# Moving the softmax's exponential, the blocks' transfers and the wo products by a slot in a fused attention and MLP kernel

## The chip, the cores and the metric

The kernel runs on one core of a Trainium2 chip. The metric is the device time of one execution in microseconds, as the median of several runs. Engines are named as in the profile: PE (TensorE matmul), PEld (TensorE weight load), DVE (VectorE), ACT (ScalarE), POOL (GpSimd) and SP (SyncE, which issues most DMAs).

## The reference

The input x has 2048 rows of 576 values, in float32. Two branches read the same normalized rows and are added to x: sliding attention with 32 heads of 18 values, in which each row looks at itself and seven rows before it in steps of two, and an MLP of 4608 hidden values with relu.

```python
xn = layernorm(x)
qkv = (xn @ wqkv).reshape(B, S, 3, 32, 18)              # q, k, v by head
idx = pos[:, None] - arange(8) * 2                      # rows s, s-2, ..., s-14
logits = where(idx >= 0, q . k[idx] * 18 ** -0.5, -1e9)
o = softmax(logits) . v[idx]
return x + o.reshape(B, S, 576) @ wo + maximum(xn @ w1, 0) @ w2
```

## The kernel before

**Tiling and phases.** The rows are dealt out in two phases (even and odd rows, so that the dilated window becomes a plain one). A phase has 8 tiles of 128 rows, and two tiles make a block of 256 rows (`tb`). The 4608 hidden values are 12 chunks (`c`) of three groups of 128 (`f`, C = 3). One slot is one combination (phase, chunk, block, f): 144 slots a phase, 288 in all, `n` in the code. A slot of the steady state has half of the hidden products of two slots (`h_two`: first half at even n, second half at odd n, then ReLU on ScalarE into `hhi` and the remainder on VectorE into `hlo`), and the output products of its own (`o_two`, into four PSUM tiles `po`). At f = 2 VectorE adds the four `po` tiles to x (line 702), and the next slot, with f = 0, uses the same tiles again. Every value is split into a high and a low float32r part, so that weights pass through a staging tile `st`, a ScalarE copy (line 161) and a VectorE subtraction (line 165): a *split*. `run_splits` does the splits that are due and calls `stage_more`, which keeps three more loads under way (`AHEAD`) in five staging buffers.

**Attention.** Heads are taken in four units of 8 heads, 24 slots apart. `qkv_tile` puts the q, k, v products of one tile into one slot, eight slots a unit. After that `attention` fills a queue `bg` of VectorE work: products q*k and their sums, the mask on GpSimd after the last sum, then maximum, subtraction, exponential (ScalarE, in the same function as the subtraction), sum, reciprocal, division, and the products with v and their sums. At the end of each slot `run_bg` takes work from that queue as long as VectorE's planned clock `t["dve"]` isn't past TensorE's planned clock `t["pe"]` by more than `margin(n)`. Both clocks are the kernel's own bookkeeping when it is built; they only set the order of instructions.

**The wo products.** In chunk 10 the attention's output tiles are transposed: `wo_a` transposes 32 by 32 blocks on VectorE and sends them by four DMAs to DRAM (`blocks_out`), `wo_f` reads them back in turned order (tile `xn`), `wo_s` splits them, and `o_two` takes wo's products in the slot with f = 1 of that block. `WO_STEPS` holds the slots for `wo_a`, `wo_f` and `wo_s`.

**The change of phase.** During chunk 11 of the first phase the second phase's first four tiles go the same way (`XT_STEPS`: load, statistics, `norm_turned`, `xt_a`, `xt_f`, `xt_s`); the last four are normalized by `stats` and `norm` and transposed on TensorE (`make_xt`).

**What sets the order.** Each engine runs its instructions in the order of the program. Work is put into a slot's list by `at` (before the slot's output products) or by `late` (after them, before `run_bg`). SP's DMAs stand in one queue in the order of the same calls: an issue that waits for its data or its buffer holds up all that follow. The pools that matter: `ph` and `pm` two PSUM tiles each, `po` four, `st` five, `pr` two, `tr` two, `xn` three.

Of the kernel before, what the change touches and what calls it, by code (L numbers as in the profile page):

```python
# [18 lines left out]
P = 128  # L19
# [7 lines left out]
C = 3  # L27
# [5 lines left out]
WO_CHUNK = 10  # L33

XT_STEPS = (
    (-6, 0, 1, 2, 4, 7),
    (-5, 1, 2, 3, 5, 8),
    (-3, 2, 3, 4, 6, 10),
    (3, 4, 5, 6, 8, 11),
)  # L40
WO_STEPS = ((-5, -4), (-3, -3), (-1, -1))
HEADW = (-9, -8, -7, -6, -5, -4)
FIRST = 4

# [14 lines left out]
def tile_body(ctx: ExitStack, tc: tile.TileContext, x, wqkv, wo, w1, w2, out):  # L59
# [61 lines left out]
    def mm_rows(runs, behind=None):  # L121


        if behind is not None:
            tc.add_manual_dep(nc.tensor.nop().ins, behind.ins.name, SYNC, reason="PSUM banks change rows")
        for pair in zip(*runs, strict=True):
            for z, (o, l, r, start, stop, n) in zip((slice(0, 64), slice(64, P)), pair):
                ins = nc.tensor.matmul(o, l[z], r[z], start=start, stop=stop)  # L128
            t["pe"] += pair[0][5] / 2400.0 + 0.002
        return ins  # L130

    def dve(n):
# [2 lines left out]

    tasks = deque()
    staged = deque()
    AHEAD = 3

    def split_task(step, load, split):  # L140
        tasks.append((step, load, split))

    def stage_more(ahead=AHEAD):
        while tasks and len(staged) < ahead:
            step, load, split = tasks.popleft()
            st = stp.tile([P, 640], F32, name="st")
            load(st)
            staged.append((step, split, st))
# [200 lines left out]
    LOWER, LOWER_MORE = FULL_K + [(4, 4)], FULL_K + [(4, 4), (4, 9)]  # L349
    UPPER, UPPER_MORE = FULL_K + [(4, 4)], FULL_K + [(4, 4), (9, 9)]  # L350

    def blocks_out(td, tr):
        for r in range(4):
            rows = slice(32 * r, 32 * r + 32)
            nc.sync.dma_start(  # L355
                td[:, :, rows].rearrange("g j i -> j g i"),
                tr[rows, :].rearrange("j (g i) -> j g i", i=32),
            )
# [8 lines left out]
    def xt_a(ph, i):  # L367

        xn, tr = XN.pop((ph, i))
        nc.vector.transpose(tr, xn)  # L370
        dve(D)
        TD[ph, i] = turned.tile([D // 32, 32, P], F32, name="words")
        blocks_out(TD[ph, i], tr)

    def xt_f(ph, i):
        tb, h = divmod(i, 2)
        if h == 0:
            XT[ph, tb] = xtp.tile([P, 10, TBN], F32R, name="xT")
        z, td = f32(XT[ph, tb][:, 0:5, h * P : (h + 1) * P]), TD.pop((ph, i))
        nc.sync.dma_start(z[:, 0:KT], td[0 : 4 * KT].rearrange("(k c) j i -> (c j) k i", k=KT))  # L380
        for rows in slice(0, DR), slice(DR, P):
            nc.sync.dma_start(z[rows, KT], td[4 * KT : D // 32].rearrange("c j i -> (c j) i"))
# [21 lines left out]
    def qkv_tile(ph, u, i):  # L404

        if u == 0 and i == 0:
            QO[ph] = qop.tile([P, NI, D], F32, name="qo")
        if i == 0:
            assert len(bg) < 38, len(bg)
            KK[ph, u] = kp.tile([P, W - 1 + NI, UD], F32, name="k")  # L410
            VV[ph, u] = vp.tile([P, W - 1 + NI, UD], F32, name="v")
            nc.gpsimd.memset(KK[ph, u][0:1, 0 : W - 1, :], 0.0)
            nc.gpsimd.memset(VV[ph, u][0:1, 0 : W - 1, :], 0.0)
        k, v, wq = KK[ph, u], VV[ph, u], WQ[ph, u]
        tb, second = i // 2, i % 2 == 1
        xt = XT[ph, tb]

        def run(h, terms):
            return [
                (PQ[h], xt[:, a, h * P : (h + 1) * P], wq[:, b, :], not second and j == 0, second and j == len(terms) - 1, 3 * UD)  # L420
                for j, (a, b) in enumerate(terms)
            ]

        if not second:
            for h in range(2):
                PQ[h] = ps_m.tile([P, 3, UD], F32, name="pm")
            PQ[2] = mm_rows((run(0, LOWER_MORE), run(1, UPPER_MORE)))
            return
        mm_rows((run(1, LOWER), run(0, UPPER)), PQ[2])
        for h in range(2):  # L430
            j, pq = i - 1 + h, PQ.pop(h)
            nc.scalar.activation(k[:, W - 1 + j, :], pq[:, 1, :], AF.Copy)  # L432
            nc.scalar.activation(v[:, W - 1 + j, :], pq[:, 2, :], AF.Copy)
            nc.scalar.activation(QO[ph][:, j, u * UD : (u + 1) * UD], pq[:, 0, :], AF.Copy)
        if i == NI - 1:
            for z in (k, v):
                for a, b in HALO:
                    nc.scalar.dma_start(z[a + 1 : b + 1, 0 : W - 1, :], z[a:b, NI : NI + W - 1, :])
# [8 lines left out]
    def attention(ph, u):  # L447
# [28 lines left out]

        def sm_sub():
            nc.vector.tensor_tensor(lg, lg, spread(m), op=ALU.subtract)
            nc.scalar.activation(lg, lg, AF.Exp, scale=scale)

        def sm_sum():
# [23 lines left out]
        for i in range(0, NI, 2):  # L505
            for f in (qk_mul, qk_sum):
                for j in (i, i + 1):
                    bg.append((big, f, (j,)))
        for f in (sm_max, sm_sub, sm_sum, sm_rcp, sm_div):
            bg.append((n + 130, f, ()))  # L510
        for i in range(0, NI, 2):
            for j in (i, i + 1):
                bg.append((big, av_mul, (j,)))
# [2 lines left out]
                    bg.append((w * UD, av_add, (j, w)))  # L516

    def run_bg(margin):
        while bg and t["dve"] + bg[0][0] / 960.0 <= t["pe"] + margin:
            n, f, a = bg.popleft()  # L520
            f(*a)
            dve(n)


    OT = {}
# [1 line left out]
    def wo_a(ph, i):  # L527


        assert (ph, i) in ready, (ph, i, len(bg))  # L530
        o = QO[ph][:, i, :]
        tr = tmp.tile([P, 640], F32, name="tr", bufs=2)
        nc.vector.transpose(tr[:, 0:D], o)
        nc.vector.transpose(tr[:, D:640], o[:, KT * P : D])
        dve(D)
        dve(DR)
        TD[ph, i] = turned.tile([5 * 4, 32, P], F32, name="turned")
        blocks_out(TD[ph, i], tr)

    def wo_f(ph, i):  # L540
        OT[ph, i] = tmp.tile([P, 5, P], F32R, name="xn", bufs=3)
        nc.sync.dma_start(f32(OT[ph, i]), TD.pop((ph, i)).rearrange("(k c) j i -> (c j) k i", k=5))

    def wo_s(ph, i):

# [88 lines left out]
    def o_two(n):  # L634


        ph, c, tb, f = slots[n]
        hi, lo = H.pop(n)
        w = W2[ph, c, f]
        with_wo = c == WO_CHUNK and f == 1  # L640
        if f == 0:
            o_tiles(n)

        def run(k, h, upper):
            cs, first = slice(k * P, (k + 1) * P), k == upper
            z = [(l[:, cs], w[:, b, CUT[h]]) for l, b in ((hi, 0), (hi, 1), (lo, 0))]
            if with_wo:
                more = wo_run(ph, 2 * tb + k, h, (UPPER_MORE if upper else LOWER_MORE) if first else (UPPER if upper else LOWER), upper)
                z = z + more
            return [  # L650
                (PO[k, h], l, r, f == 0 and first and j == 0, f == C - 1 and not first and j == len(z) - 1, CUT[h].stop - CUT[h].start)
                for j, (l, r) in enumerate(z)
            ]

        for j in range(4):
            k, h = divmod(j, 2)
            behind = PB[j - 2] if j > 1 else PB[3] if j == 0 and f else None
            PB[j] = mm_rows((run(k, h, False), run(1 - k, h, True)), behind)
        if with_wo:
            for k in range(2):  # L660
                OT.pop((ph, 2 * tb + k))
        o_out(n, rows=True)
# [59 lines left out]
    for ph in range(NPH):  # L722
# [13 lines left out]
            late(s + NI + 1, attention, ph, u)  # L736
        plan.append((b + WO_CHUNK * SPC - 6, wo_tasks, (ph,)))
        for i in range(NI):
            z = b + WO_CHUNK * SPC + C * (i // 2) + 1
            out_at, in_at, parts_at = (z + k[i % 2] for k in WO_STEPS)  # L740
            late(out_at, wo_a, ph, i)
            late(in_at, wo_f, ph, i)
            at(parts_at, wo_s, ph, i)
        if ph + 1 < NPH:
            e = b + SPP - SPC
            for i in range(NI):
                if i >= len(XT_STEPS):
                    z = e + 3 + 2 * i - (i == NI - 1)
                    at(z - 6, load_x, ph + 1, i)
                    late(z - 2, stats, ph + 1, i)  # L750
                    late(z - 1, norm, ph + 1, i)
                    at(z + 1, make_xt, ph + 1, i)
                    busy_m.add(z + 1)
                    continue
                load, first, second, send, back, parts = (e + k for k in XT_STEPS[i])
                at(load, load_x, ph + 1, i)
                late(first, stats, ph + 1, i, False, True)
                late(second, norm_turned, ph + 1, i)
                late(send, xt_a, ph + 1, i)
                at(back, xt_f, ph + 1, i)  # L760
                at(parts, xt_s, ph + 1, i)
    for step, f, a in sorted(plan, key=lambda z: z[0]):
# [87 lines left out]
    def margin(n):  # L850

        odd, qkv = n % 2 == 0, n + 1 in busy_m
        if slots[n][3] == 1:
            return (1.5 if odd else 2.4) + 2.4 * qkv
        return (2.2 if odd else 3.2) + 2.4 * qkv

    for n in range(FIRST, len(slots)):
        run_splits(n)
        g = n - n % 2 + LAG
        if n < ROW0:  # L860
# [43 lines left out]
```

## Time and profile before

| | us |
|---|---|
| median of 3 runs | 1178.96 (1178.94 to 1181.94) |
| the profiled execution | 1178.85 |
| its span on the core | 1177.1 |
| busy in that span: PE / PEld | 1153.4 / 1140.9 |
| busy in that span: DVE / ACT / POOL | 805.3 / 288.1 / 44.0 |

The span is the time from the first to the last instruction; the execution's own time has 1.75 us around it. Times in the profile's timelines count from the start of the span: start, duration, engine, line, operation, output and inputs, count; in brackets the idle time before, and who ended it. Rows of equal instructions that follow each other are merged. Instructions of one engine overlap a little, so the next start, not start plus duration, is when the engine goes on. PEld rows overlap PE rows.

### The profile page before, as it was taken

The page shows a single profiled execution, that of the slowest core. Times are in us where ns is not written, and L with a number is a line of the kernel's source. Part 1 is how long each engine was busy: PE and PEld are TensorE (multiplying, and loading weights), DVE is VectorE, ACT ScalarE, POOL GpSimd, SP SyncE. Part 2 cuts the span into 40 slices and gives each one's busy share as a digit, 9 for nine tenths or more (in the row PEclk, how much of TensorE's full clock was granted, in tenths as well). Part 3 has the DMA queues.
Part 4 walks back from the last instruction along what each step waited for, and adds up shares of the span by engine and source line. Part 5 has one row for each costly group of instructions (what it writes and reads, how often), then busy time and mean ns, then how long its engine had stood idle before and what let it go on. Part 6 is the DMA issues. An engine that isn't in the chain of part 4 may idle for free.

```text
span 1177.1 us, 38332 instructions
## 1 busy us (share of the span) xinstructions
PE 1153.4 (98%) x17114; PEld 1140.9 (97%) x17114; DVE 805.3 (68%) x1457; ACT 288.1 (24%) x756; POOL 44.0 (4%) x60
## 2 busy tenths in 40 slices
PE   9999999999999999999999999999999999998998
PEld 8999999999999999899989999999999999998998
DVE  7428787877786877763673388778778867776533
ACT  5322222121222221221442122122212212221210
POOL 3200000000000000000010000000000000000000
PEclk9999999999999999999999999999999999999999
DMA  5312222311221211744651122122213212116412
GB/s 182 98 40 60 73 55 57 83 56 47 72 65 53 72 36 50 163 82 117 148 182 57 56 61 66 44 74 66 56 57 81 56 58 66 54 43 155 90 35 82
DMA packets 149941, 89.72 MB, mean 76 GB/s; under 512 B 58528, under 2 KB 133536, under 8 KB 149776
## 3 DMA queue, kind: packets, MB, share of 16 engines
q1 hardware_dynamic: 146816, 78.61, 25.3%
q10 hardware_dynamic: 2960, 8.65, 2.5%
q8 instruction: 135, 2.21, 0.8%
q14 instruction: 30, 0.25, 0.1%
HBM read 67.90 MB, written 11.14 MB: 67 GB/s over the span
## 4 chain that ended last, share of the span: by engine, by line
PE 91%; DVE 3%; DMA 2%; SPq 1%; issue 1%; ACT 1%; POOL 0%; DVEq 0%; POOLq 0%; ACTq 0%
PE po L128 40%; PE pm L128 27%; PE ph L128 22%; DMA st<-in_w 1%; DMA xn<-turned 1%; PE po L118 1%; DVE x L702 1%; DVE w1t L165 1%; SPq L355 0%; PE po L109 0%; PE pm L302 0%; PE ph L118 0%; DVE hlo L593 0%; SPq L177 0%; DVE xT L310 0%
## 5 line engine op out<-in xcount | busy, mean ns | idle before, releaser
L128 PE MATMUL po<-w2t,hhi 64*128 64x256 f32 (+1 forms) x4448 | 452.6, 292 | 3.2 <-DVE x L702 3.2
L128 PEld LDWEIGHTS po<-w2t,hhi 64*128 64x128 f32 x4448 | 365.6, 184 | 6.8 <-issue 3.4
L128 PE MATMUL po<-w2t,hlo 64*128 64x256 f32 (+1 forms) x2224 | 341.4, 290 | 0.0
L128 PE MATMUL ph<-xT,w1t 64*128 64x256 f32 x4698 | 302.8, 275 | 10.3 <-DVE hlo L593 10.2
L128 PEld LDWEIGHTS ph<-xT,w1t 64*128 64x128 f32 x4698 | 290.3, 184 | 13.6 <-DVE hlo L593 12.3
L702 DVE TENSOR_TENSOR x<-po,x 128x320 f32<-128x320 f32 (+1 forms) x384 | 149.0, 450 | 153.1 <-PE po L128 150.2
L128 PEld LDWEIGHTS po<-w2t,hlo 64*128 64x128 f32 x2224 | 225.0, 185 | 0.0
L128 PE MATMUL pm<-wq,xT 64*128 64x432 f32 x1728 | 180.5, 354 | 0.0
L128 PE MATMUL pm<-xT,w1t 64*128 64x256 f32 x2808 | 178.3, 274 | 1.3 <-ACT w1t L161 1.3
L128 PEld LDWEIGHTS pm<-xT,w1t 64*128 64x128 f32 x2808 | 172.0, 184 | 1.8 <-ACT w1t L161 1.8
L128 PEld LDWEIGHTS pm<-wq,xT 64*128 64x128 f32 x1728 | 162.6, 184 | 2.0
L590 ACT ACTIVATE hhi<-ph 128x256 fp32r<-128x256 f32 x183 | 60.6, 381 | 296.1 <-PE ph L128 263.4
L593 DVE SCALAR_TENSOR_TENSOR hlo<-ph,hhi 128x256 fp32r<-128x256 f32 x183 | 69.3, 419 | 92.7 <-ACT hhi L590 92.7
L590 ACT ACTIVATE hhi<-pm 128x256 fp32r<-128x256 f32 x105 | 34.6, 381 | 246.7 <-PE pm L128 246.6
L463 DVE TENSOR_TENSOR pr<-qo,k 128x1152 f32<-128x1152 f32 x64 | 85.6, 1350 | 1.8 <-DMA k<-k 1.8
L493 DVE TENSOR_TENSOR pr<-lg,v 128x1152 f32<-128x1152 f32 x64 | 85.1, 1350 | 0.2
L466 DVE TENSOR_REDUCE lg<-pr 128x64 f32<-128x1152 f32 x64 | 85.1, 1343 | 0.0
L593 DVE SCALAR_TENSOR_TENSOR hlo<-pm,hhi 128x256 fp32r<-128x256 f32 x105 | 39.7, 419 | 50.3 <-ACT hhi L590 48.9
L432 ACT ACTIVATE k<-pm 128x144 f32<-128x144 f32 x64 | 19.3, 301 | 223.3 <-PE pm L128 223.3
L500 DVE TENSOR_TENSOR pr<-pr 128x288 f32<-128x288 f32 (+1 forms) x128 | 70.9, 599 | 0.0
L165 DVE TENSOR_TENSOR w1t<-st,w1t 128x640 fp32r<-128x640 f32 x70 | 57.2, 817 | 13.3 <-ACT w1t L161 12.8
L165 DVE TENSOR_TENSOR w2t<-st,w2t 128x576 fp32r<-128x576 f32 x72 | 54.0, 750 | 17.4 <-ACT w2t L161 17.4
(87 smaller groups left out, 698.3 us busy)
## 6 DMA issues: line engine op xcount, KB each, us to landing
st<-in_w SPq DMA_DIRECT2D x72, 288.0 KB, 2.9
st<-in_w SPq DMA_DIRECT2D x72, 256.0 KB, 3.0
st<-in_wqkv SPq DMA_DIRECT2D x32, 216.0 KB, 3.0
turned<-tr SPq DMA_DIRECT2D x64, 80.0 KB, 2.9
xn<-turned SPq DMA_DIRECT2D x16, 320.0 KB, 3.8
st<-in_w SPq DMA_DIRECT2D x144, 32.0 KB, 2.7
out<-x SPq DMA_DIRECT2D x15, 288.0 KB, 2.4
x<-in_x SPq DMA_DIRECT2D x14, 288.0 KB, 4.5
```

Source lines behind the costliest of these rows:

```text
L118: nc.tensor.matmul(o, l, r, start=start, stop=stop)
L128: ins = nc.tensor.matmul(o, l[z], r[z], start=start, stop=stop)
L165: nc.vector.tensor_tensor(lo, src, f32(hi), op=ALU.subtract)
L432: nc.scalar.activation(k[:, W - 1 + j, :], pq[:, 1, :], AF.Copy)
L463: nc.vector.tensor_tensor(pr[i], q, window(k, i), op=ALU.mult)
L466: nc.vector.tensor_reduce(lg[:, i], pr.pop(i).rearrange(heads, d=Dh), axis=AX.X, op=ALU.add)
L493: nc.vector.tensor_tensor(pr[i].rearrange(heads, d=Dh), e, window(v, i).rearrange(heads, d=Dh), op=ALU.mult)
L500: nc.vector.tensor_tensor(o, z[:, 0:n], z[:, n : 2 * n], op=ALU.add)
L590: nc.scalar.activation(hi, pt, AF.Relu)
L593: nc.vector.scalar_tensor_tensor(lo, pt, 0.0, f32(hi), op0=ALU.max, op1=ALU.subtract)
L702: nc.vector.tensor_tensor(acc[:, cols], PO[k, h], acc[:, cols], op=ALU.add)
```

## The change

- **Exponential.** It becomes a step of its own in the queue (`sm_exp`), booked at no VectorE time. `run_bg` doesn't take it in a call that has already run something, so it stands at the end of a slot after that of the subtraction.
- **Transfers of turned blocks.** `xt_a` and `wo_a` only transpose; `blocks_out` is a step of its own in the next slot.
- **wo products.** They are taken in the slot with f = 2 instead of f = 1; `WO_STEPS` is written anew for it.
- **Norms of the second phase's last four tiles.** `stats` and `norm` move from the end of a slot to the middle of the next.
- **Loads.** From slot 8 on, four loads are kept under way instead of three.
- **The planner.** A pair of row-split matmuls of n columns is booked at n * 17/16 / 2400 + 0.001 us instead of n / 2400 + 0.002; `margin` is 0.3 higher, and 0.8 lower for each split due by the next slot.

```diff
-    (-6, 0, 1, 2, 4, 7),
-    (-5, 1, 2, 3, 5, 8),
-    (-3, 2, 3, 4, 6, 10),
-    (3, 4, 5, 6, 8, 11),
+    (-6, 0, 1, 2, 3, 4, 7),
+    (-5, 1, 2, 3, 4, 5, 8),
+    (-3, 2, 3, 4, 5, 6, 10),
+    (3, 4, 5, 6, 7, 8, 11),
 )
-WO_STEPS = ((-5, -4), (-3, -3), (-1, -1))
+WO_STEPS = ((-5, -4, -3, -1), (-4, -3, -2, -1))
...
-            t["pe"] += pair[0][5] / 2400.0 + 0.002
+            t["pe"] += pair[0][5] * 17 / 16 / 2400.0 + 0.001
...
-    AHEAD = 3
+    AHEAD = {"n": 3}
...
-    def blocks_out(td, tr):
+    def blocks_out(ph, i):
+        td, tr = TD[ph, i]
...
         def sm_sub():
             nc.vector.tensor_tensor(lg, lg, spread(m), op=ALU.subtract)
+
+        def sm_exp():
             nc.scalar.activation(lg, lg, AF.Exp, scale=scale)
...
-        for f in (sm_max, sm_sub, sm_sum, sm_rcp, sm_div):
-            bg.append((n + 130, f, ()))
+        for f in (sm_max, sm_sub, sm_exp, sm_sum, sm_rcp, sm_div):
+            bg.append((0 if f is sm_exp else n + 130, f, ()))
...
-        while bg and t["dve"] + bg[0][0] / 960.0 <= t["pe"] + margin:
+        ran = False
+        while bg and t["dve"] + bg[0][0] / 960.0 <= t["pe"] + margin and not (ran and bg[0][0] == 0):
             n, f, a = bg.popleft()
             f(*a)
-            dve(n)
+            if n:
+                ran = True
+                dve(n)
...
-        with_wo = c == WO_CHUNK and f == 1
+        with_wo = c == WO_CHUNK and f == C - 1
...
-            z = b + WO_CHUNK * SPC + C * (i // 2) + 1
-            out_at, in_at, parts_at = (z + k[i % 2] for k in WO_STEPS)
-            late(out_at, wo_a, ph, i)
-            late(in_at, wo_f, ph, i)
-            at(parts_at, wo_s, ph, i)
+            z = b + WO_CHUNK * SPC + C * (i // 2) + C - 1
+            turn, send, back, parts = (z + k for k in WO_STEPS[i % 2])
+            late(turn, wo_a, ph, i)
+            late(send, blocks_out, ph, i)
+            (at if i % 2 else late)(back, wo_f, ph, i)
+            at(parts, wo_s, ph, i)
...
-                    late(z - 2, stats, ph + 1, i)
-                    late(z - 1, norm, ph + 1, i)
+                    at(z - 1, stats, ph + 1, i)
+                    at(z, norm, ph + 1, i)
...
-                late(send, xt_a, ph + 1, i)
+                late(turn, xt_a, ph + 1, i)
+                at(send, blocks_out, ph + 1, i)
...
+        due = sum(z[0] <= n + 1 for z in (*staged, *tasks))
         if slots[n][3] == 1:
-            return (1.5 if odd else 2.4) + 2.4 * qkv
-        return (2.2 if odd else 3.2) + 2.4 * qkv
+            return (1.8 if odd else 2.7) + 2.4 * qkv - 0.8 * due
+        return (2.5 if odd else 3.5) + 2.4 * qkv - 0.8 * due
...
     for n in range(FIRST, len(slots)):
+        if n == ROW0:
+            AHEAD["n"] = 4
```

More of the change, by code (lines that the diff above doesn't have):

```diff
@@ L137, in tile_body, with stage_more @@
     staged = deque()
-    AHEAD = 3
+    AHEAD = {"n": 3}
     def split_task(step, load, split):
         tasks.append((step, load, split))
-    def stage_more(ahead=AHEAD):
-        while tasks and len(staged) < ahead:
+    def stage_more(ahead=None):
+        while tasks and len(staged) < (ahead or AHEAD["n"]):
             step, load, split = tasks.popleft()
@@ L371, in xt_a @@
         dve(D)
-        TD[ph, i] = turned.tile([D // 32, 32, P], F32, name="words")
-        blocks_out(TD[ph, i], tr)
+        TD[ph, i] = turned.tile([D // 32, 32, P], F32, name="words"), tr
     def xt_f(ph, i):
@@ L378, in xt_f @@
             XT[ph, tb] = xtp.tile([P, 10, TBN], F32R, name="xT")
-        z, td = f32(XT[ph, tb][:, 0:5, h * P : (h + 1) * P]), TD.pop((ph, i))
+        z, td = f32(XT[ph, tb][:, 0:5, h * P : (h + 1) * P]), TD.pop((ph, i))[0]
         nc.sync.dma_start(z[:, 0:KT], td[0 : 4 * KT].rearrange("(k c) j i -> (c j) k i", k=KT))
@@ L408, in qkv_tile @@
         if i == 0:
-            assert len(bg) < 38, len(bg)
+            assert len(bg) < 39, len(bg)
             KK[ph, u] = kp.tile([P, W - 1 + NI, UD], F32, name="k")
@@ L536, in wo_a @@
         dve(DR)
-        TD[ph, i] = turned.tile([5 * 4, 32, P], F32, name="turned")
-        blocks_out(TD[ph, i], tr)
+        TD[ph, i] = turned.tile([5 * 4, 32, P], F32, name="turned"), tr
     def wo_f(ph, i):
         OT[ph, i] = tmp.tile([P, 5, P], F32R, name="xn", bufs=3)
-        nc.sync.dma_start(f32(OT[ph, i]), TD.pop((ph, i)).rearrange("(k c) j i -> (c j) k i", k=5))
+        nc.sync.dma_start(f32(OT[ph, i]), TD.pop((ph, i))[0].rearrange("(k c) j i -> (c j) k i", k=5))
     def wo_s(ph, i):
@@ L754, in tile_body @@
                     continue
-                load, first, second, send, back, parts = (e + k for k in XT_STEPS[i])
+                load, first, second, turn, send, back, parts = (e + k for k in XT_STEPS[i])
                 at(load, load_x, ph + 1, i)
```

## The prediction

> **What bounds the kernel now.** I read the page first, then the list of waits, then a table of windows, and then the timeline of each engine where a window shows idle time.
>
> ```profile
> PE 1153.4 (98%) x17114; PEld 1140.9 (97%) x17114; DVE 805.3 (68%) x1457; ACT 288.1 (24%) x756; POOL 44.0 (4%) x60
> ```
>
> TensorE is the bound, and the change leaves its instructions as they are, so only its idle time can be won. PEld, the weight loads, is the better ledger: matmul ends are modelled and hide the first part of a stall.
>
> ```profile
> ACT lg L479 <- DVE lg L478: 53.0, 8, 7.9
> PEld ph L128 <- DVE hlo L593: 12.3, 8, 1.7
> DVE m L475 <- POOL lg L469: 10.3, 8, 1.6
> ```
>
> ScalarE stands in front of the softmax's exponential eight times, up to 7.9 us each, and the weight loads wait eight times for `hlo`. The windows (length, then PE, PEld, DVE, ACT, POOL busy) say where:
>
> ```profile
> 133.00:150.00 17.00, 15.60 (x218) 15.09 (x218) 12.61 (x19) 4.20 (x12) 2.86 (x3) 1.00 0.21 58
> 150.00:428.00 278.00, 275.21 (x4127) 274.19 (x4126) 216.48 (x359) 62.59 (x182) 5.71 (x6) 1.00 0.22 59
> 428.00:448.00 20.00, 19.32 (x304) 18.85 (x302) 16.02 (x28) 5.70 (x12) 1.09 (x1) 1.00 0.28 78
> 474.00:504.00 30.00, 27.57 (x414) 26.23 (x412) 21.44 (x42) 5.91 (x12) 0.00 (x0) 1.00 0.68 152
> 570.00:616.00 46.00, 44.11 (x659) 41.95 (x657) 33.08 (x78) 20.67 (x47) 5.91 (x8) 1.00 0.68 185
> 616.00:1010.00 394.00, 389.82 (x5813) 387.01 (x5811) 281.40 (x469) 91.27 (x265) 8.57 (x9) 1.00 0.22 60
> 1010.00:1030.00 20.00, 19.58 (x310) 19.12 (x308) 16.42 (x28) 5.70 (x12) 1.09 (x1) 1.00 0.28 78
> 1055.00:1085.00 30.00, 26.56 (x398) 25.39 (x397) 20.63 (x42) 6.65 (x14) 0.00 (x0) 1.00 0.68 151
> ```
>
> PEld idle is length less busy: 1.91 around one softmax (unit 0 of the first phase); 3.81 for units 1 and 2; 1.15 at unit 3; 3.77 at the first wo products; 4.05 at the change of phase; 6.99 for units 0 to 2 of the second phase (three times 1.9 and 1.3 of small waits); 0.88 at its unit 3; 4.61 at its first wo products. That is 27.2 us, and all that the change can reach.
>
> **The exponential, units 0 to 2 of each phase (six times).** Timelines around the first:
>
> ```profile
> 126.88 1.35 DVE L463 TENSOR_TENSOR pr<-qo,k 128x1152 f32<-128x1152 f32 x1
> ...
> 137.76 1.14 DVE L475 TENSOR_REDUCE m<-lg 128x64 f32<-128x512 f32 x1 [1.21 <-POOL lg L469]
> 138.94 0.69 DVE L478 TENSOR_TENSOR lg<-lg,m 128x512 f32<-128x512 f32 x1
> 140.39 1.14 DVE L482 TENSOR_REDUCE r<-lg 128x64 f32<-128x512 f32 x1 [0.76 <-ACT lg L479]
> 141.44 0.82 DVE L165 TENSOR_TENSOR w1t<-st,w1t 128x640 fp32r<-128x640 f32 x1
> 142.16 0.76 DVE L593 SCALAR_TENSOR_TENSOR hlo<-ph,hhi 128x256 fp32r<-128x256 f32 x2
> ```
>
> ```profile
> 139.72 0.63 ACT L479 ACTIVATE lg<-lg 128x512 f32<-128x512 f32 x1 [7.84 <-DVE lg L478]
> ```
>
> ```profile
> 140.94 0.30 PE L128 MATMUL po<-w2t,hlo 64*128 64x320 f32 x2
> 142.65 2.21 PE L128 MATMUL ph<-xT,w1t 64*128 64x256 f32 x28 [1.40 <-DVE hlo L593]
> ```
>
> TensorE is done with its products at 141.0 and needs both `ph` banks; `hlo` frees them at 142.9. Two queues hold `hlo` up: on ScalarE the exponential stands ahead of the weight split and of `hhi`; on VectorE subtraction, the wait for the exponential, and the sum stand ahead of the weight split and `hlo`.
>
> The order of instructions of the changed kernel shows, in all six places: the slot before ends in q*k product 7, sums 6 and 7 and the maximum; then come the weight split and `hlo`; the subtraction follows; one slot later come exponential, sum, reciprocal, division. So ahead of `hlo` 138.94 to 141.44, 2.50 us, is taken out. But the planner now charges 0.8 us for each due split and holds back one product that ran two slots earlier: 1.35 is put in. `hlo` comes 2.50 - 1.35 = 1.15 earlier and the stall falls from 1.91 to 0.76, not to zero, since the wait for GpSimd's mask (1.21) stays in that queue. Six times 1.15 is **6.9 us**. Ends: nothing (the product takes the whole place, `hhi` is no hindrance) and 1.91 each (11.5). The value is nearest to rows of this very queue. The exponential's new place costs nothing: behind the q, k, v copies of its slot, while VectorE is at the output sums, which end with the slot; if that cover went, the sum would wait the 0.76 it waits today, with no `hlo` behind it.
>
> [...] The rows show the bank's reader late, not the bank scarce: in other slots the same two banks come free in time. [...]
>
> **Unit 3 (twice).** No q, k, v products run beside it and the sums of f = 2 are what is late.
>
> ```profile
> 427.51 2.60 DVE L466 TENSOR_REDUCE lg<-pr 128x64 f32<-128x1152 f32 x2
> ...
> 435.64 1.15 DVE L482 TENSOR_REDUCE r<-lg 128x64 f32<-128x512 f32 x1 [0.76 <-ACT lg L479]
> 436.72 0.80 DVE L165 TENSOR_TENSOR w1t<-st,w1t 128x640 fp32r<-128x640 f32 x1
> 437.45 1.53 DVE L702 TENSOR_TENSOR x<-po,x 128x256 f32<-128x256 f32 x4
> ...
> 440.25 0.53 DVE L485 RECIPROCAL r<-r 128x64 f32<-128x64 f32 x1
> ```
>
> In the new order one of the two reductions (1.30) has run a slot earlier, the wait of 0.76 is gone, and the reciprocal (0.53) is put in: the sums start 1.5 us earlier than 437.45, more than TensorE waits for them. The whole 1.15 and 0.88 go: **2.0 us** (0 to 2.0).
>
> **The first wo products (twice).** They need two output tiles, each through a VectorE transpose, four transfers out, one transfer back and a split.
>
> ```profile
> 476.97 2.02 SPq L355 DMA_DIRECT2D turned<-tr  x4
> 482.77 2.25 SPq L355 DMA_DIRECT2D turned<-tr  x4
> 487.46 1.10 SPq L542 DMA_DIRECT2D xn<-turned  x2
> ```
>
> ```profile
> turned<-tr SPq DMA_DIRECT2D x64, 80.0 KB, 2.9
> xn<-turned SPq DMA_DIRECT2D x16, 320.0 KB, 3.8
> ```
>
> ```profile
> 479.65 0.71 DVE L165 TENSOR_TENSOR v<-st,wq 128x576 fp32r<-128x576 f32 x1
> ```
>
> ```profile
> 492.60 0.74 ACT L551 ACTIVATE k<-xn 128x640 fp32r<-128x640 f32 x1 [0.34 <-DMA xn<-turned]
> ```
>
> ```profile
> 492.31 0.38 PE L128 MATMUL po<-wq,k 64*128 64x256 f32 x1
> ```
>
> Now: SP sits at 476.97 waiting for the transposes while weight loads queue behind; these loads come late (about 2.5 us of the 3.77), and the tiles cost the rest. With four staged loads, and transfers out behind the loads, the weights are there: that part goes. But wo's product also moves one slot (3.1 us) on, so TensorE asks for the tiles at 492.3 as before. When do they come? SP's new order is: two weight loads of three DMAs, transfers out of tile 0, one load, tile 0 back, transfers out of tile 1, one load, tile 1 back; each return waits for its transfers' landing, and the next ones stand behind it. At 0.5 us an issue (2.02 for four): the second weight load waits for the staging buffer that the split at 479.65 frees; that split ends at 480.4 today and at about 479.8 then (one tile's transposes, 0.9, no longer ahead of it, a small sum of 0.3 is), so the load's issues end at 481.4; tile 0 out to 483.5, landed at 485.9 (last issue plus 2.9); back 0.5; tile 1 out to 488.5, landed 490.9; back issued, landed 494.7 (3.8); split 0.74: 495.4. That is 3.1 us after 492.3, and the second half of the split adds 0.3. With landings up to 1 us longer, as neighbours on a busy queue have, it is 5.4. I take 4.2 for each phase, against 3.77 and 4.61: **0 us** won (ends: 4 won, 4 lost). The stall changes its cause, not its size. The later three wo blocks have a 10 us slot between transfers and use; they stay covered.
>
> [...]
>
> **The change of phase.** Two stalls: slots 144 and 148 of the program, both `hlo` late.
>
> ```profile
> 593.51 0.63 ACT L389 ACTIVATE xT<-xT 128x512 fp32r<-128x512 f32 x1
> ...
> 594.26 2.34 PE L128 MATMUL ph<-xT,w1t 64*128 64x256 f32 x28 [0.98 <-DVE hlo L593]
> ```
>
> ```profile
> 607.49 0.57 DVE L288 TENSOR_SCALAR xn<-x,mv,rstd 128x576 f32<-128x576 f32 x1
> 607.98 0.81 DVE L266 BATCH_NORM_STATS2 bst<-x 128x6 f32<-128x288 f32 x2
> 609.68 0.75 DVE L593 SCALAR_TENSOR_TENSOR hlo<-ph,hhi 128x256 fp32r<-128x256 f32 x2
> 610.15 2.20 PE L128 MATMUL ph<-xT,w1t 64*128 64x256 f32 x28 [0.87 <-DVE hlo L593]
> ```
>
> At 148 the norm and the statistics (607.49 to 609.15, 1.66) move behind `hlo`: the stall goes, 0.87 on PE and about 1.3 with the refill. At 144 late weights go too, but the norm of tile 4 now stands behind tile 3's split, whose data still comes near 593.5 (ScalarE's half 0.63, VectorE's about 1.0, the norm 0.57: 595.9 and a little). TensorE, without a stall, would be ready for its transposes 1.4 before that; today it loses 0.98 and the refill, about 1.6, there. Together **1.5 us** (0 to 3.3).
>
> **Sum.** 6.9 + 2.0 + 0 + 1.5 = 10.4 of 27.2 us. The profiled execution took 1178.85 with a span of 1177.1, and the median of three is 1178.96: forecast 1168.5.
>
> **The rivals.**
> A. The tiles arrive earlier too (SP finds its buffers free sooner; 1.7 lost at each wo instead of 4.2) and `hlo` is in time: 5.0 and 6 x 0.76 = 4.6 more, 1159. For it: DMA share is 0.2 outside these windows; against: the chain of landings is serial.
> B. The gaps at the exponential stay: product, mask's wait and maximum take the place of what left the queue, and the two banks are as late as before: 1178.9 - 3.5 = 1175.4. Against it: 2.50 us leave the queue and 1.35 enter.
> C. Tiles sent a slot later arrive a slot later: 3.1 us more at each first wo block and at the change of phase: 1168.5 + 9.3 = 1177.8.
> D. Slower: the planner's TensorE clock runs 5% faster than before, so VectorE is given background work with no reserve; from 0.12 us of delay of `hlo` in each of some 90 pairs of slots (8 units of about 11), the 10.4 us are spent, and at 0.25 the time is 1168.5 + 22 = 1190. Against it: a product that the plan books at 1.335 us follows its neighbour after 1.30 in the row at 427.51, and the charge for due splits gives slack back.
> E. The change doesn't do what it says: the order of instructions shows the exponential moved in all eight units; hardly any chance.
>
> **Numbers.** Forecast 0.60, A 0.14, B 0.08, C 0.09, D 0.08, E 0.01. A change under 0.3% (3.5 us) can't be told from none. Faster: forecast, A, and about all of B's better half and C's better tail, 0.82; same 0.10; slower 0.08. The range goes from A's value, 1159, to between B and C, 1176: left out are C's worse part, D and the far end of A.
>
> **What would show it.** Right: the wait of ScalarE for the subtraction falls from 53 us to a few; PEld waits for `hlo` fall from 12.3 to about 6, six of them near 0.7; no wait for the sums near units 3; the first wo products wait about 4 us for tile data, not for weights; VectorE's norm precedes a wait at slot 144 alone. Wrong: `hlo` waits in many slots of the attention (D); wo waits over 7 us (C); `hlo` waits unchanged (B).

## The result and the profile after

The changed kernel takes 1172.22 us (median of 4 runs, 1171.2 to 1173.83); beside it the kernel before took 1180.45 us (4 runs, 1178.94 to 1182.44). The ratio is 0.9931, with an interval of 0.9908 to 0.9953. The profiled execution took 1171.2 us, its span 1169.5 us; the forecast was 1168.5. The change is a gain, as forecast, but of 7.6 us in the profiled execution instead of 10.4 (8.2 by the medians above).

The engines' line of the page after:

```profile
PE 1152.5 (99%) x17114; PEld 1142.7 (98%) x17114; DVE 804.8 (69%) x1457; ACT 287.7 (25%) x756; POOL 43.4 (4%) x60
```

TensorE still has the same 17114 matmuls. The list of waits after (engine, line, who was waited for, total us, times, longest):

```profile
ACT k L558 <- DMA xn<-turned: 10.8, 4, 5.5
...
ACT xT L391 <- DMA xT<-words: 4.3, 2, 3.2
...
ACT lg L483 <- DVE lg L480: 0.9, 2, 0.6
```

And that of the weight loads alone:

```profile
PEld po L129 <- ACT k L558: 7.9, 2, 4.2
PEld ph L129 <- ACT xT L391: 3.1, 1, 3.1
PEld ph L129 <- DVE hlo L600: 1.7, 6, 0.3
```

ScalarE's 53 us of waits for the subtraction (`lg`) have fallen to 0.9. The weight loads waited 12.3 us for `hlo`; now they wait 1.7, six times at most 0.3. In their place stand two waits for the turned output tiles (`k`, 7.9) and one for the turned tiles of the second phase (`xT`, 3.1); behind both ScalarE waits for the transfers back. The windows of after, around the same work as those of before (length, then PE, PEld, DVE, ACT, POOL busy; then granted clock, DMA share, GB/s):

```profile
132.00:148.00 16.00, 16.00 (x224) 15.49 (x222) 10.41 (x17) 3.65 (x12) 2.86 (x3) 1.00 0.23 64
148.00:425.00 277.00, 276.91 (x4154) 275.88 (x4153) 222.10 (x365) 62.87 (x183) 5.71 (x6) 1.00 0.22 59
425.00:445.00 20.00, 20.00 (x328) 19.96 (x326) 18.00 (x32) 5.70 (x12) 1.09 (x1) 1.00 0.29 81
...
472.00:503.00 31.00, 26.98 (x409) 26.77 (x406) 14.65 (x33) 5.01 (x12) 0.00 (x0) 0.94 0.62 137
...
567.00:613.00 46.00, 42.99 (x609) 40.39 (x607) 31.26 (x75) 19.36 (x47) 4.84 (x8) 0.96 0.62 168
613.00:1005.00 392.00, 391.90 (x5855) 389.28 (x5853) 284.07 (x475) 91.69 (x266) 9.09 (x10) 1.00 0.22 61
1005.00:1025.00 20.00, 20.00 (x330) 20.00 (x330) 17.87 (x30) 5.70 (x12) 1.09 (x1) 1.00 0.29 78
...
1050.00:1080.00 30.00, 26.49 (x405) 26.28 (x403) 16.81 (x36) 5.80 (x12) 0.00 (x0) 0.94 0.67 150
```

PEld idle (length less busy) falls at the exponentials and at unit 3: 1.91 to 0.51, 3.81 to 1.12, 1.15 to 0.04, 6.99 to 2.72, 0.88 to 0. It rises at the first wo products (3.77 to 4.23) and at the change of phase (4.05 to 5.61), and falls at the second phase's first wo products (4.61 to 3.72). New between these two executions is the clock: 0.94, 0.96 and 0.94 in the three windows that hold the long waits, where before had 1.00.

Idle time doesn't show what the lower clock costs (1.5 to 1.7 us behind each of the three waits, read further below). The matmuls are the same and, apart from the wo products, which come a slot later, in the same order. So the start of the first, the second, the k-th matmul can be compared in the two traces; how the distance grows from one place to the next is what TensorE gained there:

| place | forecast gain | measured gain |
|---|---|---|
| six exponentials (units 0 to 2) | 6.9 | 8.1 (1.25 to 1.45 each) |
| unit 3, twice | 2.0 | 2.8 (1.40, 1.36) |
| first wo products, phases 1 and 2 | 0 | -1.2, +0.25 |
| change of phase | 1.5 | -3.1 |
| all the rest | 0 | 0.4 |
| sum | 10.4 | 7.2 |

The span shrank by 7.6; what the sum lacks lies behind the last matmul, since the first one starts at 1.35 in both.

### The profile page after: what moved, and what is told of

It reads as the page before. It is cut to its first block, busy times and chain, and to the rows that moved or that the text cites. A ratio compares the mean times of both kernels' runs of the same rounds, so it can differ in the third digit from the quotient of the medians.

```text
span 1169.5 us, 38344 instructions
## 1 busy us (share of the span) xinstructions
PE 1152.5 (99%) x17114; PEld 1142.7 (98%) x17114; DVE 804.8 (69%) x1457; ACT 287.7 (25%) x756; POOL 43.4 (4%) x60
## 4 chain that ended last, share of the span: by engine, by line
PE 93%; DMA 3%; SPq 1%; DVE 1%; ACT 1%; issue 1%; DVEq 0%; POOL 0%; ACTq 0%
PE po L129 40%; PE pm L129 27%; PE ph L129 22%; PE ph L119 1%; PE po L119 1%; DMA turned<-tr 1%; SPq L358 1%; DMA words<-pr 1%; DMA xn<-turned 1%; PE pm L303 1%; DVE x L709 0%; DMA xT<-words 0%; DMA x<-in_x 0%; DVE hlo L600 0%; SPq L179 0%
```

## The experiments

In what follows "gain" is always that comparison of matmul starts with the kernel before, in us. Each profile is of one execution; medians and intervals stand where there are any.

**One part alone: the exponential.** The kernel before, with the exponential as a step of its own and nothing else of the change:

```diff
+        def sm_exp():
             nc.scalar.activation(lg, lg, AF.Exp, scale=scale)
...
+            bg.append((0 if f is sm_exp else n + 130, f, ()))
...
+        while bg and ... and not (ran and bg[0][0] == 0):
```

> Only the exponential is a step of its own, one slot later; planner, transfers, wo products, norms and loads as before. Theory 1 (the exponential's place on ScalarE and the sum's wait on VectorE hold hlo up): the subtraction stays ahead of hlo, the wait and the sum leave, 1.84 us of the 2.50; no product is put in. So each of the six stalls of 1.9 us falls to 0.1 to 0.4: about 1168.5 us, 10 below the kernel before. Stalls at the first wo products and at the change of phase stay as before (3.8, 4.1, 4.6 us). Theory 2 (the gain at the exponential comes from the planner's new clock and margins, which hand out VectorE's work otherwise): the six stalls stay near 1.9, time within 3 us of before.

One run took 1164.12 us (span 1162.3) beside 1181.92 for the kernel before on the same chip: less than the whole change took. The gain at the six exponentials is 1.83 to 2.00 each, 11.6 in all, so nothing is left of those stalls. VectorE around the first one:

```profile
137.57 1.15 DVE L475 TENSOR_REDUCE m<-lg 128x64 f32<-128x512 f32 x1 [1.21 <-POOL lg L469]
138.76 0.69 DVE L478 TENSOR_TENSOR lg<-lg,m 128x512 f32<-128x512 f32 x1
139.37 0.82 DVE L165 TENSOR_TENSOR w1t<-st,w1t 128x640 fp32r<-128x640 f32 x1
140.10 0.75 DVE L598 SCALAR_TENSOR_TENSOR hlo<-ph,hhi 128x256 fp32r<-128x256 f32 x2
140.77 1.16 DVE L484 TENSOR_REDUCE r<-lg 128x64 f32<-128x512 f32 x1
```

The subtraction is still ahead of the weight split and `hlo`; only the wait for the exponential and the sum have gone from there, and that is enough.

**One part alone: the planner.** The kernel before with the new clock rate and the new margins:

```diff
-            t["pe"] += pair[0][5] / 2400.0 + 0.002
+            t["pe"] += pair[0][5] * 17 / 16 / 2400.0 + 0.001
...
+        due = sum(z[0] <= n + 1 for z in (*staged, *tasks))
-            return (1.5 if odd else 2.4) + 2.4 * qkv
-        return (2.2 if odd else 3.2) + 2.4 * qkv
+            return (1.8 if odd else 2.7) + 2.4 * qkv - 0.8 * due
+        return (2.5 if odd else 3.5) + 2.4 * qkv - 0.8 * due
```

> Only the planner's TensorE clock and the margins of the changed kernel, the rest as before. Theory 1: the exponential is still behind the subtraction in the same slot, so the six stalls remain, between 1.5 and 3 us each, since one product is put into the same queue; the stalls of unit 3 may move; time 1176 to 1184. Theory 2: the six stalls fall to about 0.5 us each, time near 1170.

1172.65 us (span 1170.9) beside 1181.92. At the exponentials it gains 1.28 to 1.45 each, as much as the whole change, with the exponential where it was; at unit 3 nothing (-0.02 and -0.39). I had not expected the first. Its VectorE rows say how:

```profile
138.98 1.15 DVE L475 TENSOR_REDUCE m<-lg 128x64 f32<-128x512 f32 x1 [1.21 <-POOL lg L469]
140.06 0.80 DVE L165 TENSOR_TENSOR w1t<-st,w1t 128x640 fp32r<-128x640 f32 x1
140.79 0.73 DVE L593 SCALAR_TENSOR_TENSOR hlo<-ph,hhi 128x256 fp32r<-128x256 f32 x2
141.46 0.67 DVE L478 TENSOR_TENSOR lg<-lg,m 128x512 f32<-128x512 f32 x1
142.88 1.16 DVE L482 TENSOR_REDUCE r<-lg 128x64 f32<-128x512 f32 x1 [0.76 <-ACT lg L479]
```

The charge for due splits pushes subtraction, exponential and sum behind `hlo`. The changed kernel has the same rows at the same distance (maximum at 138.87, `hlo` at 140.67). Either part alone takes most or all of the stall away, and at these six places together they are worth no more than the weaker: the planner's part also brings the maximum 1.3 us later than in the kernel with the exponential alone (138.87 against 137.57), by the q*k product that it holds back (1.35), and so leaves some 0.55 us of stall in each place.

**The change of phase: the transfers in their old place.** The changed kernel, in which the second phase's first tiles are sent at the end of the slot of their transposes, as before:

```diff
-                at(send, blocks_out, ph + 1, i)
+                late(turn, blocks_out, ph + 1, i)
```

> The changed kernel, but at the change of phase the transfers stand with the transposes again (blocks_out right after xt_a), the rest as changed. Theory 1 (a slot's delay of the sends puts each tile's sends behind the return of the tile before on SP's queue, and the chain of landings makes tile 3 late): the wait of 3.1 us for xT at the first slot of the second phase goes or falls under 0.5, and the lower clock after it (3.4 us at half speed, about 1.6 us) goes too: 4 to 5 us below the changed kernel, about 1167. Theory 2 (tile 3 is late because four loads under way stand ahead of the transfers): the wait stays above 2 us and the time near 1172.

1166.66 us (span 1164.9) beside 1181.92. At the change of phase it gains 1.85 where the changed kernel loses 3.1. ScalarE has no wait in front of tile 3's split at 589.35, and SP shows why. First SP's queue in the changed kernel (outward transfers into `words`, returns into `xT`):

```profile
562.24 2.12 SPq L358 DMA_DIRECT2D words<-pr  x4
...
566.21 0.38 SPq L382 DMA_DIRECT2D xT<-words  x1
...
567.84 2.91 SPq L358 DMA_DIRECT2D words<-pr  x4
573.04 0.38 SPq L382 DMA_DIRECT2D xT<-words  x1
...
574.72 2.20 SPq L358 DMA_DIRECT2D words<-pr  x4
...
579.98 0.38 SPq L382 DMA_DIRECT2D xT<-words  x1
...
582.29 2.39 SPq L358 DMA_DIRECT2D words<-pr  x4
...
588.45 0.38 SPq L382 DMA_DIRECT2D xT<-words  x1
```

And with the transfers in their old place:

```profile
563.16 2.13 SPq L358 DMA_DIRECT2D words<-pr  x4
...
565.95 2.49 SPq L358 DMA_DIRECT2D words<-pr  x4
568.60 0.40 SPq L382 DMA_DIRECT2D xT<-words  x1
...
571.35 2.19 SPq L358 DMA_DIRECT2D words<-pr  x4
...
579.12 3.04 SPq L358 DMA_DIRECT2D words<-pr  x4
...
584.44 0.38 SPq L382 DMA_DIRECT2D xT<-words  x1
```

In the changed kernel each outward transfer stands behind the return of the tile before it, and a return waits for its own tile to land in DRAM: out, back, out, back, one after the other (SP's waits for the landing: 4.9 us in four, the longest 2.2). In the old place tile 1 is on its way out before tile 0's return is reached, and the last return starts 4 us earlier (584.44 against 588.45).

**The first wo products: their two tiles two slots earlier.** The changed kernel with

```diff
+            if i < 2:
+                turn, send, back = turn - 2, send - 2, back - 2
```

> The changed kernel, but transposes, sends and returns of the first wo block's two tiles stand two slots earlier in each phase. Theory 1 (the wait at the first wo products is the serial chain transposes, sends, landing, return, landing, split, and has no other cause): two slots are 6.2 us, so the waits of 4.6 and 4.1 us go, and with them the lower clock after each (about 1.6 us): 11 us below the changed kernel, about 1161. Theory 2 (SP's queue of loads, which wait for staging buffers, holds the transfers to the same time however early they are asked for): the waits shrink by less than 2 us, time 1168 or above.

1159.96 us (span 1158.2) beside 1181.92. The waits for `k` are gone from the list of the weight loads, and the two places gain 4.4 and 5.2 us:

```profile
472.00:500.00 28.00, 28.00 (x450) 28.00 (x448) 17.56 (x38) 7.20 (x15) 0.00 (x0) 1.00 0.68 159
```

So the whole stall was tile data, and the weights were no hindrance. The change of phase, untouched here, still loses 2.2, with a wait of 2.6 for `xT`.

**The number of loads ahead.** The changed kernel with three loads kept under way instead of four:

```diff
-            AHEAD["n"] = 4
+            AHEAD["n"] = 3
```

> The changed kernel with three loads under way as before. Theory 1 (the prediction's: two weight loads that stand ahead of tile 0's sends on SP make the tiles of the first wo block late): the wait for tile data shrinks from 4.6 by 1 to 3 us in each phase; weights may come late again at the change of phase. Theory 2 (the slot's delay of the sends and the return in between make them late, whatever the loads): the wait stays within 0.7 us of 4.6 and 4.1.

1169.94 us (span 1168.2) beside 1180.73 for the kernel before. With one load less in the queue the tiles come earlier and weights later:

```profile
PEld ph L129 <- DVE hlo L600: 5.6, 7, 3.8
PEld po L129 <- ACT k L558: 4.9, 2, 2.5
```

The waits for `k` fall from 7.9 to 4.9 in sum, so the fourth load costs the two tiles' chain 1.2 to 1.8 us each. At the change of phase a wait of 3.8 for `hlo` takes the place of the 3.1 for `xT`, probably since there the weights are late, and that stage loses 4.2 instead of 3.1. On balance the difference to the changed kernel (1.3 in span) is of the size that single runs differ by.

**The clock at the first wo products.** The changed kernel with 24 transposes of the identity into a free PSUM tile just before the first block's wo products, so that TensorE has work while it waits; the transposes are extra work:

```diff
+        if with_wo and tb == 0:
+            keep_warm(n)
```

> The changed kernel with 24 extra 128-column transposes of the identity (about 2.6 us, into a PSUM tile that nobody reads) in front of the first wo block's products of each phase, so that TensorE works for part of the 4.2 us in which it waits for tile 1. Nothing of the computation is left out. Theory 1 (the time after that wait is lost to the lower granted clock, 3.4 us at half): no lower clock at the two wo waits, each wo stage 1.5 us shorter although the tiles come no earlier, 3 us below the changed kernel, about 1169; the lower clock at the change of phase stays. Theory 2 (what is lost after the wait is the refill of TensorE's pipeline): the wo stages stay as long, time near 1172.

1173.5 us (span 1171.8) beside 1180.73, no better than the changed kernel (1171.2 to 1173.83).

```profile
472.00:506.00 34.00, 32.49 (x492) 31.80 (x491) 18.54 (x39) 6.72 (x14) 0.00 (x0) 1.00 0.61 134
567.00:616.00 49.00, 44.92 (x636) 42.46 (x634) 33.16 (x80) 20.07 (x48) 4.95 (x8) 0.97 0.59 160
1050.00:1082.00 32.00, 30.33 (x437) 29.64 (x435) 16.79 (x36) 5.80 (x12) 0.00 (x0) 0.95 0.64 143
```

The clock stayed at 1.00 at the first place and not at the second (0.95). The 24 transposes take 2.84 us of TensorE's time in each phase. Most of that lies in the waits, which shrink from 4.23 and 3.72 to 1.71 and 1.87; the later wait at the change of phase grew to 4.3 us. So this way of filling the wait doesn't pay; what the clock alone costs is read from other runs, below.

**Both repairs together.** The changed kernel with the second phase's transfers in their old place and the first two wo tiles two slots earlier (the two diffs above):

> The changed kernel with both repairs together: sends at the change of phase right behind the transposes, the first wo block's two tiles two slots earlier. If the two waits are independent, the two gains add: 18.5 + 4.9 less than the kernel before by the ledger of TensorE's lag, near 1155 us; if they share SP's queue, one gives part back: 1158 or more. Six stalls of about 0.5 us for hlo remain.

1155.92 us (4 runs, 1155.54 to 1156.66), 0.9789 of the kernel before [0.9767, 0.9811].

```profile
472.00:500.00 28.00, 28.00 (x451) 27.91 (x449) 17.48 (x38) 7.07 (x15) 0.00 (x0) 1.00 0.68 158
560.00:606.00 46.00, 45.99 (x680) 43.82 (x678) 33.28 (x80) 21.53 (x50) 5.35 (x8) 1.00 0.67 181
1050.00:1080.00 30.00, 30.00 (x482) 30.00 (x481) 17.05 (x36) 5.34 (x11) 0.00 (x0) 1.00 0.61 134
```

The three places lose nothing worth the name, and the granted clock is 1.00 in all of them. What is left are the six remainders at the exponentials.

**The same from the other side.** The kernel before with the exponential's step, four loads ahead, the norms' new places and its first two wo tiles two slots earlier; planner, wo products and transfers as before:

> The kernel before (its planner, its transfers, wo at f = 1) with the exponential as a step of its own, four loads under way, the second phase's last norms in the middle of the slot, and the first wo block's tiles two slots earlier. Theory: with the old planner the six stalls for hlo go to zero instead of 0.5, and the first wo block has its tiles and its weights in time: 14.8 + 10 less than before by the ledger, near 1154 us. Rival: wo's tiles come in time, but weights behind the transposes on SP are late again, 1158 or more.

1161.25 us (4 runs, 1159.05 to 1162.72), ratio 0.9834 [0.9812, 0.9856]. The exponentials' stalls are zero again (1.86 to 1.90 won each), the change of phase gains 2.0, but the first wo products gain only 0.2 and 1.1:

```profile
475.44 0.74 ACT L161 ACTIVATE w1t<-st 128x640 fp32r<-128x640 f32 x1 [2.18 <-DMA st<-in_w]
...
478.44 0.68 ACT L161 ACTIVATE w2t<-st 128x576 fp32r<-128x576 f32 x1 [2.27 <-DMA st<-in_w]
```

Here ScalarE waits for weights (2.18 and 2.27 us), which came late behind the transfers on SP (out from 465.62 to 469.1, back from 472.21 to 473.3), and VectorE's sums come late, at 480.50, behind the splits at 476.21 and 479.16. TensorE's waits there are 2.43 and 2.20 us, and its clock is at half for 3.4 us after each. With the wo products at f = 1 the tiles' transfers and the weights ask for SP at the same time: loads stand between those transfers, from 469.17 on, and behind them, from 473.36 on. That the later slot of the changed kernel (f = 2) is what makes room for both is likely, but not shown: the two kernels differ in the planner and the transfers too.

**The last remainder.** Both repairs, and slots 0 to 87 of each phase with the old planner again:

```diff
-            t["pe"] += pair[0][5] * 17 / 16 / 2400.0 + 0.001
+            t["pe"] += pair[0][5] * (17 / 16 if NEW[0] else 1) / 2400.0 + (0.001 if NEW[0] else 0.002)
...
+        if not NEW[0]:
+            return (1.5 if odd else 2.4) + 2.4 * qkv if slots[n][3] == 1 else (2.2 if odd else 3.2) + 2.4 * qkv
...
+        NEW[0] = n % SPP >= 88
```

> The version with the old order of the blocks' transfers and with the first wo products taken a block's length earlier (best1), in which slots 0 to 87 of each phase also go back to the old planner (old clock rate of TensorE, old margins, no charge for due splits); the later slots keep the new one. The exponential stays a step of its own. Theory 1: what is left of each of the six stalls at an exponential (about 0.55 us with the new planner) is the product and the mask's wait that the new planner leaves ahead of hlo; with the old planner they stood at zero (exp_only). Expect six times 0.5 = 3 us less than best1's 1155.9, about 1152.7, no waits of the weight loads for hlo near the exponentials of units 0 to 2. Theory 2: the 0.55 us belong to the blocks' and loads' order, which exp_only lacks too: expect them unchanged, about 1155.9. Under both the stalls at unit 3, at the first wo products and at the change of phase stay as in best1.

1152.88 us (4 runs, 1152.2 to 1154.7), ratio 0.9767 [0.9742, 0.9792]; span 1150.4. The six places gain 1.83 to 2.04 each, the wo products 4.25 and 5.56, the change of phase 1.93. No wait for `hlo` stands in the list of the weight loads any more. This is the fastest version, 19 us below the changed kernel.

## Why the prediction was right, and where it failed

**The exponential: right, somewhat too small.** The step held that 2.50 us leave VectorE's queue ahead of `hlo` and a held-back product puts 1.35 in. The stall fell to about 0.55 instead of 0.76, which makes 8.1 instead of 6.9. Both halves were shown: the exponential alone, without the held-back product, takes the stall to zero, and the last version does so in the changed kernel. What the prediction did not see is that the new planner alone takes out as much. Rival B (the gaps stay) fell: with the same two banks the gaps shrank to 0.55, and to nothing in the kernel with the exponential alone.

**Unit 3: right, and above its bound.** 1.40 and 1.36, together 2.8, against 2.0, which was to be the most: the idle time of the weight loads (1.15 and 0.88), from which that bound was taken, showed less than these two stalls cost. The planner alone gains nothing there and the exponential's step alone 1.69 and 1.36, so it is the step. Around the first of the two, VectorE has the same order with the planner alone as in the changed kernel, but its weight split at 429.58 waits 1.39 us for ScalarE's copy, which stands behind the exponential.

**The first wo products: wait and cause right, its second cost missed.** The step gave 4.2 us of wait for the tile data. SP, and then TensorE, in the changed kernel:

```profile
476.28 2.27 SPq L358 DMA_DIRECT2D turned<-tr  x4
478.65 0.48 SPq L190 DMA_DIRECT2D st<-in_w  x1
480.34 0.38 SPq L549 DMA_DIRECT2D xn<-turned  x1
480.81 2.64 SPq L358 DMA_DIRECT2D turned<-tr  x4
...
487.00 0.38 SPq L549 DMA_DIRECT2D xn<-turned  x1
```

```profile
490.91 0.92 PEld L129 LDWEIGHTS po<-wq,k 64*128 64x128 f32 x7 [4.23 <-ACT k L558]
```

It is the chain that was written down, out, back, out, back, and 4.23 us (3.72 in the second phase). But the first place lost 1.2 us in all: after the wait the granted clock was at half for 3.4 us. The price of that shows beside the version with early tiles, matmul by matmul: the distance jumps by 4.3 us at this wait, grows by another 1.6 until the clock is full again at 494.2, and then stays. At the second place, beside the version with both repairs, it is 3.8 and 1.5. In the run with the second phase's transfers in their old place the same wait (4.18) was followed by 6.8 us at half, and the distance to the changed kernel grows by 1.1 more. That the forecast of 0 came out so near is in part luck: the clock was left out, but the kernel before lost more here than its idle time shows as well (early tiles win 4.4 us where 3.77 was idle).

**The change of phase: the step that failed.** The prediction wrote that at slot 144 tile 3's "data still comes near 593.5", and forecast 1.5 us won. It had seen for the first wo products that a later send makes a serial chain on SP, and did not walk through the same queue here, although the transfers out were moved behind the returns in the same way. In the changed kernel, 4.1 us ahead by then, 593.5 is 589.4; the data came at 591.5:

```profile
591.52 0.63 ACT L391 ACTIVATE xT<-xT 128x512 fp32r<-128x512 f32 x1 [3.19 <-DMA xT<-words]
```

```profile
592.20 0.53 PEld L129 LDWEIGHTS ph<-xT,w1t 64*128 64x128 f32 x8 [3.12 <-ACT xT L391]
```

Nor was it the transposes of tile 4 that TensorE was to wait at, as the step had it, but already the hidden products ahead of them, which need tile 3. The part on slot 148 held: no wait for `hlo` is left there. Undoing the transfers' move alone turns 3.1 lost into 1.85 won, close to the forecast 1.5. Of the difference 3.1 us are the wait and 1.7 the lower clock behind it, read in the same way beside the version with both repairs. Rival C, the tiles that come a slot later, was true in this one place and not in the other two: it was priced as one mechanism for three places, and should have been weighed for each.

**Rivals A and D fell.** A: the tiles came no earlier, and TensorE waited 4.23 and 3.72 us for them instead of 1.7. D: the weight loads waited 1.7 us in all for `hlo`, against 10 that would have spent the gain. (The row at 427.51 that the prediction sets against D is of two q*k sums, not of a product; the plan books both alike, so the argument stands.)

By its sizes: of the 3.2 us that the sum of 10.4 was too high, the change of phase makes 4.6 and the first wo products 1.0 (one place lost 1.2, the other won 0.25); the exponentials, unit 3 and the rest gave 2.4 back.

## What to carry to other kernels

On SP's queue a transfer out, its return, and the next transfer out formed one chain here (the last return started at 588.45, against 584.44 with the transfers in their old place); when any of them moves by a slot, write down the whole queue in its new order for every place where the pattern occurs, not for one. A planner that is changed together with the order it plans hides what each part does: here the exponential's step alone was worth more than the whole change. Three waits of the bounding engine cost more than their length here, through the clock that was granted after them (1.5 to 1.7 us a time).

## What the runs showed of the hardware

The clock was not expected to fall. In the changed kernel the trace has TensorE's granted clock at half (0.50) for 3.4 us from 490.8, 593.2 and 1071.1 on: at the end of a wait of 4.23, 1.0 us after the end of one of 3.12, and near the end of one of 3.72. The kernel before, whose longest such wait was 1.9, had 1.00 in all its windows.

The clock fell with shorter waits as well: in the kernel with the exponential alone the longest wait near the first wo products was 1.4 us, and the window there has 0.94. Its list of waits, and that window:

```profile
PEld po L128 <- issue: 2.6, 4, 1.4
```

```profile
472.00:503.00 31.00, 29.82 (x444) 29.35 (x442) 22.68 (x47) 6.70 (x13) 0.00 (x0) 0.94 0.67 148
```

Waits of 1.7 to 1.9 us stand beside either clock. With the 24 transposes the wait of 1.71 at the first wo products lies in a window at 1.00, and that of 1.87 at the second in one at 0.95; the longest of the kernel before for its output tiles, 1.9 at its second wo products, lies in a window at 1.00:

```profile
PEld po L128 <- ACT k L551: 3.1, 3, 1.9
```

So in these runs the length of a wait doesn't tell by itself whether the clock falls, and what does is not shown.

The kernel before, too, has a lower clock in other executions: those timed beside the other runs took 1178.39 to 1184.11 us at mean granted clocks of 1.000 down to 0.995, the profiled one 1178.85 at 1.000. So its clock was full in that execution, but not in every one; why, no trace here shows.
